# Half of a one-megabyte weight load is sent behind the last value block, and two row products trade places with a turned sum

## The chip, the cores and the metric

The kernel runs on one core of a Trainium2 chip, in one launch. Its time is the device time of one execution in microseconds (us). One execution was also recorded by the hardware profiler. Times inside the trace are counted from the first recorded instruction, and the span runs to the last one.

## The reference

One token goes through two branches that are mixed by a gate `g`:

```
g   = sigmoid(sum(x * gate_w))
q   = x @ wq                                  # 32 heads of 128, x has 512 elements
p   = softmax(q . k_cache / sqrt(128))        # 4096 cached keys for each head
a   = (p . v_cache).reshape(4096) @ wo        # 4096 -> 512
h   = relu(x @ w1 + b1) ** 2                # 512 -> 1376
b   = h @ w2 + b2                             # 1376 -> 512
out = g * a + (1 - g) * b                     # 512 numbers, bf16
```

Both branches read the same `x`. Keys and values are 32 MB each in bf16, and with the weights the core reads 78 MB. Nothing is reused, so every byte is brought in once.

## The kernel before

**Blocks.** The 32 heads are handled in 8 groups of 4. For each group there is a key block K0 to K7 and a value block V0 to V7 of 4 MB each. They pass through four slots of the tile `KV` in the order `K0 K1 V0 K2 K3 V1 K4 V2 K5 K6 V3 K7 V4 V5 V6 V7`. V7 alone is brought in as four transfers of 1 MB with a semaphore each (`V_PARTS`), so that its products can start on the first quarter. Each part is 8 KB in each of 128 partitions.

**The queue.** Nearly all transfers are issued by SyncE (SP), written out by hand in the function under `@block.sync`. The end of that list is what the change edits. Before it, `load_w2(0)` is issued just ahead of V7. It brings rows 0 to 7 of `w2a`, 8 KB for each partition. After V7 come `wob` (rows of `wo` for the last eight heads, 1 MB), `wox` (128 KB, `wo` for head 23) and the three small pieces of `w2`:

```
W2_PARTS = [(0, 8), (FG, FG + 1), (8, 9), (9, 10)]
```

Here `FG` is 10. Pieces 0 to 9 are rows of `w2a` (a row is 128 x 512 weights), and piece `FG` is the remainder `w2b` with 96 partitions. `w2` is thus ten full parts and a short one, and each entry of `W2_PARTS` has its own semaphore `s_w2[n]`.

**The products at the end.** TensorE runs, in program order, `den(6)` and `pv(6)` (128 matmuls on V6), `mlp_out(0)` (32 matmuls on `w2a` rows 0 to 7), `den(7)` and `pv(7)` (128 matmuls on V7, a wait at each quarter), `regroup()` (a transpose and 16 small matmuls, with VectorE between them, that turn the last heads' outputs into columns), `out_b()` (32 matmuls on `wob`), `out_x()` (4 on `wox`) and `mlp_out(1, last=True)` (4 on `w2b`). All of these from `mlp_out(0)` on except `den`, `pv` and `regroup` add into `acc`, four columns of 128 numbers. When the last is done, VectorE adds the bias and writes `accs` (line 857).

**Turning the sum.** The output is wanted as 4 rows of 128. A matmul of `accs` with the identity turns the four columns into four rows in `acc4` (line 707, in 32-bit floats). Rows 8 and 9 of `w2` do not go through `acc`. `mlp_rows` (line 645) multiplies each of them with a diagonal arrangement `hd` of the hidden values, so that the result is in row form at once and adds into `acc4`. In the kernel before, row 8 is multiplied ahead of the turned sum and row 9 behind it. VectorE then casts `acc4` to `fin4` (line 859) and SP sends it out (line 349).

Of the kernel before, what the change touches and what calls it, by code (L numbers as in the profile page):

```python
# [5 lines left out]
def bass_gated_mix__gqa_block_cached__dense_activation_squared_relu__decode_kernel(  # L6
# [25 lines left out]
    FG = 10  # L32
# [28 lines left out]
    K_PARTS = [[4]] * NQ  # L61
    V_PARTS = [[4]] * (NQ - 1) + [[1, 1, 1, 1]]
    QF = 4
    W2_PARTS = [(0, 8), (FG, FG + 1), (8, 9), (9, 10)]
    INNER, OUTER, SEAM, WRAP = range(4)
    RUNS = [(INNER, 4, 12, 0, 2), (INNER, 4, 12, 1, 2),
            (OUTER, 4, 3, 0, 1), (SEAM, 7, 2, 0, 1), (OUTER, 9, 7, 0, 1),
# [18 lines left out]
    def turns():  # L86
        at, out = 0, []
        for _, e, k, _, _ in RUNS:
            d = (e - at) % 16
            out.append((False, d) if d != 1 else (True, e))  # L90
            at = (e + k) % 16
        return out
# [24 lines left out]
    with ctx:  # L117
        def sb(name, shape, dt):
            return ctx.enter_context(nc.sbuf_tensor(name, shape, dt))
# [4 lines left out]
        def sem(name):  # L124
            return ctx.enter_context(nc.semaphore(name))
# [31 lines left out]
        identf = sb("identf", [128, 128], fp32)  # L157
# [25 lines left out]
        accs = sb("accs", [128, 4], fp32)  # L183
# [18 lines left out]
        acc4 = pO[0:4, 128:256]  # L202
# [11 lines left out]
        s_w1 = sem("s_w1")  # L214
        s_w2 = [sem(f"s_w2{n}") for n in range(len(W2_PARTS))]
        s_wo = sem("s_wo")
# [54 lines left out]
        s_fin = sem("s_fin")  # L271
# [21 lines left out]
        @block.sync  # L293
        def _(eng):
            def load(dst, src, slot, parts, sems):
                at = 0
                for n, s in zip(parts, sems):
                    a, b = at * PB * 128, (at + n) * PB * 128
                    eng.dma_start(dst[:, slot, a:b], src[:, a:b]).then_inc(s, 16)
                    at += n  # L300

            def load_kv(n):
                kind, q = ORDER[n]
                if n >= 4:
                    done(*ORDER[n - 4])
                if kind == "K":
                    load(KV, k_q[q, :, :], n % 4, K_PARTS[q], s_k[q])
                else:
                    load(KV, v_q[q, :, :], n % 4, V_PARTS[q], s_v[q])

            def done(kind, q):
                if kind == "K":
                    eng.wait_ge(s_sd, q + 1)
                    eng.wait_ge(s_t, GQ * (q + 1))
                else:
                    eng.wait_ge(s_pv, q + 1)

            def load_first(n):
                if n == 0:
                    eng.wait_ge(s_qps, NQ)  # L320
                p, st, k, q = STRIPS[len(RUNS) + n]
                eng.dma_start(W2[p:p + st * (k - 1) + 1:st, :, :], woa_v[q:q + k, :, :],
                              max_dma_last_dim=16384).then_inc(s_wr, 16)

            def load_w2(n):
                a, b = W2_PARTS[n]
                if a < FG:
                    eng.dma_start(w2a[:, a:b, :], w2_v[:, a:b, :]).then_inc(s_w2[n], 16)
                else:
                    eng.dma_start(w2b[:, :], B_w2[FG * 128:F, :]).then_inc(s_w2[n], 16)  # L330

            for n in range(len(ORDER)):
                if n == len(ORDER) - 1:
                    load_w2(0)
                load_kv(n)
                if n == 2:
                    eng.wait_ge(s_z, 1)
                    eng.wait_ge(s_b2, 1)
                    eng.dma_start(w1_sb[:, :, :], w1_v[:, :, :]).then_inc(s_w1, 16)
                if 4 <= n < 4 + len(FIRST):  # L340
                    load_first(n - 4)
            done("V", NQ - 4)
            eng.dma_start(wob_sb, wob_v).then_inc(s_wo, 16)
            eng.dma_start(wox, A_wo[HX * 128:NA * 128, :]).then_inc(s_wx, 16)
            load_w2(1)
            load_w2(2)
            load_w2(3)
            eng.wait_ge(s_f4, 1)
            eng.dma_start(out[0, 0, :].rearrange("(j p) -> j p", p=128), fin4[:, :]).then_inc(s_out, 16)

# [116 lines left out]
        def _(eng):  # L467
# [138 lines left out]
            def regroup():  # L606
                eng.wait_ge(s_on, NQ)
                eng.transpose(KP[0][0:NH - NA, 0:128], onorm[:, NA:NH], ident[:, :]).then_inc(s_oT, 1)
                eng.wait_ge(s_oc, 1)
                for c in range(16):  # L610
                    mm = eng.matmul(O2B, selB[:, c // 8, c % 8, :], oB[:, TB * c:TB * c + TB],
                                    start=(c == 0), stop=(c == 15))
                mm.then_inc(s_oT, 1)

            def out_b():
                eng.wait_ge(s_o2, 1)
                eng.wait_ge(s_wo, 16)
                for t in range(TB):
                    for j in range(4):
                        eng.matmul(acc[:, j:j + 1], wob_sb[:, t, j * 128:(j + 1) * 128], o2B[:, t:t + 1],  # L620
                                   start=False, stop=False, skip_group_check=True)

            def out_x():
                eng.wait_ge(s_wx, 16)
                for j in range(4):
                    eng.matmul(acc[:, j:j + 1], wox[:, j * 128:(j + 1) * 128], onorm[:, HX:HX + 1],
                               start=False, stop=False, skip_group_check=True)

            def mlp_out(c, last=False):
                eng.wait_ge(s_w2[c], 16)  # L630
                a, b = W2_PARTS[c]
                for n in range(a, b):
                    M = 128 if n < FG else FR
                    w = w2a[:, n, :] if n < FG else w2b[:, :]
                    for j in range(4):
                        mm = eng.matmul(acc[:, j:j + 1], w[:, j * 128:(j + 1) * 128], hs[0:M, n:n + 1],
                                        start=False, stop=last, skip_group_check=True)
                if last:
                    mm.then_inc(s_acc, 1)

            def mlp_rows(c):
                eng.wait_ge(s_w2[c], 16)
                n = W2_PARTS[c][0]
                for j in range(4):
                    mm = eng.matmul(acc4, hd[:, n - 8, 4 * j:4 * j + 4], w2a[:, n, j * 128:(j + 1) * 128],
                                    start=(n == 8 and j == 0), stop=(n == FG - 1 and j == 3),
                                    skip_group_check=True)
                return mm

# [49 lines left out]
            pv(NQ - 1)  # L699
            regroup()  # L700
            out_b()
            out_x()
            mlp_out(1, last=True)
            eng.wait_ge(s_hs, 3)
            mlp_rows(2)
            eng.wait_ge(s_as, 1)
            eng.matmul(acc4, accs[:, :], identf[:, :], start=False, stop=False, skip_group_check=True)
            mlp_rows(3).then_inc(s_fin, 1)


        @block.vector
# [179 lines left out]
```

## Time and profile before

| what | value |
|---|---|
| median of 3 runs | 193.93 us (193.81 to 194.0) |
| the profiled execution's own time | 193.83 us |
| its span, first to last instruction | 192.4 us |
| mean granted TensorE clock | 0.689 |
| busy share of TensorE, VectorE, ScalarE | 66%, 66%, 52% |
| HBM read | 78.32 MB, 407 GB/s over the span |
| DMA engines' mean busy share from 172.16 to 185.41 us | 1.01 |
| the same from 185.41 to 189.28 us | 0.53 |
| the same from 189.28 us to the end | 0.00 |

The profiled execution took 1.43 us more than its span, which lies outside the recorded instructions. It is 0.10 us below the median. The shares of the engines are averages over the whole span. For the change only the last 20 us count, and there the table's last three rows say how far the transfers, and not an engine, set the pace.

### The profile page before, as it was taken

The numbers are of one execution on the slowest core, as the hardware profiler recorded it, in microseconds if no ns is written. First come the engines' busy times: TensorE is split into PE (matmuls) and PEld (weight loads), VectorE is DVE, ScalarE is ACT, GpSimd is POOL, SyncE is SP. The second block draws the span as 40 slices with busy tenths as digits, with TensorE's granted clock in tenths as the row PEclk, the third lists the DMA queues.
The fourth block names the chain that finished last, engine by engine and source line by source line (L and its number), as shares of the span: only waits on it lengthen the run. The fifth ranks groups of instructions, "written<-read, shape, count | busy, mean of one in ns | idle before, by whom it ended". The sixth has DMA issues, their size and how long they took to land.

```text
span 192.4 us, 6533 instructions
## 1 busy us (share of the span) xinstructions
PE 126.4 (66%) x2439; PEld 112.6 (59%) x2441; DVE 127.9 (66%) x1120; ACT 99.2 (52%) x214; POOL 19.8 (10%) x37
## 2 busy tenths in 40 slices
PE   0049498784689946384992659278789385755646
PEld 0023376563679946374982659178689384655645
DVE  1340399999607899999989459999989981100001
ACT  3006489799502898457398029869809935000000
POOL 5000000019964300000000000000000000000000
PEclk9999759699555576755597558858856955555555
DMA  6999999999999999999999999999999999999990
GB/s 225 437 429 436 436 438 426 436 401 451 426 424 433 436 433 422 434 433 426 404 426 426 417 433 436 414 424 433 431 433 426 429 421 433 426 380 421 417 341 18
DMA packets 4975, 78.73 MB, mean 409 GB/s; under 512 B 1334, under 2 KB 1816, under 8 KB 1817
## 3 DMA queue, kind: packets, MB, share of 16 engines
q1 hardware_dynamic: 3906, 75.76, 92.8%
q0 software_dynamic: 1024, 2.56, 3.4%
q8 instruction: 19, 0.31, 0.7%
q14 instruction: 12, 0.09, 0.1%
q10 hardware_dynamic: 14, 0.01, 0.0%
HBM read 78.32 MB, written 0.00 MB: 407 GB/s over the span
## 4 chain that ended last, share of the span: by engine, by line
DMA 43%; PE 22%; DVE 17%; ACT 12%; issue 4%; SPq 1%; ACTq 0%; DVEq 0%
DMA KV<-in_A_k_cache_dram 29%; DMA KV<-in_A_v_cache_dram 14%; DVE KV L773 13%; ACT kT L418 8%; PE KP L504 6%; PE pO L548 6%; PE pQ L486 3%; ACT E L436 2%; PE pQ L561 2%; ACT qb L407 2%; PE pS L516 1%; DVE w_sb L748 1%; PE pQ L557 1%; PE pO L539 1%; DVE S L773 1%
## 5 line engine op out<-in xcount | busy, mean ns | idle before, releaser
L773 DVE CUSTOM_DVE_ANT_0 KV<-KV,qb 128x128 bf16<-128x128 bf16 x512 | 110.2, 282 | 13.7 <-DMA KV<-in_A_k_cache_dram 13.7
L418 ACT ACTIVATE kT<-KP 128x1024 bf16<-128x1024 bf16 x64 | 61.9, 1026 | 37.1 <-PE KP L504 35.7
L504 PE MATMUL KP<-ident,KV 128*128 128x128 bf16 x512 | 51.8, 271 | 5.6 <-DMA KV<-in_A_k_cache_dram 5.6
L504 PEld LDWEIGHTS KP<-ident,KV 128*128 128x128 bf16 x512 | 43.0, 125 | 7.7 <-DMA KV<-in_A_k_cache_dram 4.1
L773 DVE DVE_READ_ACCUMULATOR2_ANT S<- 128x1 f32 x512 | 39.8, 78 | 0.0
L516 PE MATMUL pS<-qcol,kT 128*128 128x4 bf16 x512 | 23.5, 168 | 24.2 <-ACT kT L418 23.7
L516 PEld LDWEIGHTS pS<-qcol,kT 128*128 128x128 bf16 x512 | 20.9, 103 | 27.0 <-ACT kT L418 26.8
L548 PEld LDWEIGHTS pO<-E,KV 128*128 128x128 bf16 x1024 | 29.4, 105 | 7.9 <-DMA KV<-in_A_v_cache_dram 7.1
L548 PE MATMUL pO<-E,KV 128*128 128x4 bf16 x1024 | 29.1, 166 | 7.4 <-DMA KV<-in_A_v_cache_dram 6.6
L436 ACT ACTIVATE E<-S,nM 32x128 bf16<-32x128 f32 x32 | 18.4, 576 | 1.0
L407 ACT ACTIVATE qb<-pQ 32x128 bf16<-32x128 f32 x20 | 5.4, 268 | 13.1 <-PE pQ L486 12.8
L795 DVE RECIPROCAL rden<-pO 128x4 f32<-128x4 f32 x7 | 1.2, 173 | 15.3 <-PE pO L548 15.3
L373 POOL DMA_DIRECT2D xb<-in_B_w_dram x9 | 5.4, 604 | 39.3 <-PE pQ L486 39.3
L424 ACT ACTIVATE S<-pS 32x64 f32<-32x64 f32 x32 | 6.9, 214 | 4.3 <-PE pS L516 3.7
L486 PE MATMUL pQ<-W,xb 128*128 128x512 bf16 x18 | 7.1, 534 | 1.7 <-ACT qcol L412 1.1
L436 ACT ACTIVATION_READ_ACCUMULATOR E<-S,nM 32x1 f32 x32 | 8.0, 250 | 0.0
L376 POOL DMA_DIRECT2D W<-in_A_wo_dram x14 | 7.9, 565 | 0.0
L476 PE MATMUL pO<-S,onesf 1*24 1x128 f32 x2 | 0.6, 409 | 9.4 <-DVE S L739 9.4
L801 DVE SCALAR_TENSOR_TENSOR onorm<-pO,gcol,rden 128x4 bf16<-128x4 f32 x8 | 1.8, 222 | 7.4 <-PE pO L548 7.1
L754 DVE TENSOR_SCALAR e<-ez 128x1 f32<-128x1 f32 x1 | 0.2, 154 | 8.5 <-ACT ez L445 8.5
L476 PEld LDWEIGHTS pO<-S,onesf 1*24 1x24 f32 x2 | 0.1, 116 | 9.5 <-DVE S L739 9.5
L528 PE MATMUL pM<-onesf,dg 1*128 1x1 f32 x16 | 3.6, 294 | 3.1 <-DVE dg L788 3.0
(108 smaller groups left out, 90.5 us busy)
## 6 DMA issues: line engine op xcount, KB each, us to landing
KV<-in_A_k_cache_dram SPq DMA_DIRECT2D x8, 4096.0 KB, 30.6
KV<-in_A_v_cache_dram SPq DMA_DIRECT2D x7, 4096.0 KB, 25.4
W<-in_A_wq_dram SPq DMA_DIRECT2D x1, 4096.0 KB, 12.2
KV<-in_A_v_cache_dram SPq DMA_DIRECT2D x4, 1024.0 KB, 23.2
W<-in_A_wo_dram POOLq DMA_DIRECT2D x2, 768.0 KB, 19.9
w_sb<-in_B_w_dram SPq DMA_DIRECT2D x1, 1376.0 KB, 11.7
w2a<-in_B_w_dram SPq DMA_DIRECT2D x1, 1024.0 KB, 30.8
KV<-in_A_wo_dram SPq DMA_DIRECT2D x1, 1024.0 KB, 28.7
```

What stands on the lines that cost most here:

```text
L373: eng.dma_start(dm[0:d, sent, :, 0:8], src[:, :, 0:8]).then_inc(s_dm[sent], 16)
L376: eng.dma_start(W2[p:p + st * (k - 1) + 1:st, :, :], woa_v[q:q + k, :, :], max_dma_last_dim=16384).then_inc(s_wp[n], 16)
L407: eng.activation(qb[rows(r), c, :], QR[c][rows(r), r * 128:(r + 1) * 128], ACT.Copy)\
L418: eng.activation(kT[:, n % NT, :], KP[n % 3][:, :], ACT.Copy).then_inc(s_ev, 1)
L424: eng.activation(S[rows(r), q % NS, 0:YQ], S2[rows(r), :, r], ACT.Copy).then_inc(s_cp, 1)
L436: eng.activation(E[rows(r), q % NE, :, r], S[rows(r), q % NS, :], ACT.Exp, bias=nM[rows(r), q:q + 1], scale=SCALE, accum_out=RS[rows(r), h ...
L486: mm = eng.matmul(QR[c], xb[:, t, :], wq_sb[:, t, c * 512:(c + 1) * 512], start=(t == 0), stop=(t == 3))
L504: mm = eng.transpose(KP[n % 3][:, y * 128:(y + 1) * 128], key(q, b), ident[:, :])
L516: mm = eng.matmul(pS[q % 2][:, R * c:R * c + R], kT[:, n % NT, y * 128:(y + 1) * 128], qcol[:, R * q:R * q + R], start=True, stop=True)
L548: mm = eng.matmul(O[:, R * q:R * q + R], KV[:, V_SLOT[q], b * 128:(b + 1) * 128], E[:, q % NE, COLUMN[b], :], start=(b == 0), stop=(b == N ...
L561: mm = eng.matmul(H[0:M, n:n + 1], lhs, xcol[:, t:t + 1], start=False, stop=(t == 3))
L773: ins = eng.tensor_tensor_reduce(key(q, b), key(q, b), qb[:, q, :], 1.0, 0.0, ALU.mult, ALU.add, S[:, q % NS, c:c + 1])
```

## The change

`w2a` rows 0 to 7 are no longer one transfer of 1 MB but two of 512 KB (4 KB for each partition). The first stays ahead of V7. The second is issued behind `wob` and ahead of `wox`. Its 16 matmuls move with it: `mlp_out(0)` keeps 16 of its 32 in front of `den(7)`, and a new `mlp_out(1)` with the other 16 stands between `out_b()` and `out_x()`. The numbers of the later entries of `W2_PARTS` rise by one. Also, row 9 of `w2` is now multiplied ahead of the turned sum, right behind row 8, and the turned sum is the last matmul of the kernel.

```
-    W2_PARTS = [(0, 8), (FG, FG + 1), (8, 9), (9, 10)]
+    W2_PARTS = [(0, 4), (4, 8), (FG, FG + 1), (8, 9), (9, 10)]
...
             eng.dma_start(wob_sb, wob_v).then_inc(s_wo, 16)
+            load_w2(1)
             eng.dma_start(wox, A_wo[HX * 128:NA * 128, :]).then_inc(s_wx, 16)
-            load_w2(1)
             load_w2(2)
             load_w2(3)
+            load_w2(4)
             eng.wait_ge(s_f4, 1)
...
             out_b()
+            mlp_out(1)
             out_x()
-            mlp_out(1, last=True)
+            mlp_out(2, last=True)
             eng.wait_ge(s_hs, 3)
-            mlp_rows(2)
+            mlp_rows(3)
+            mlp_rows(4)
             eng.wait_ge(s_as, 1)
-            eng.matmul(acc4, accs[:, :], identf[:, :], start=False, stop=False, skip_group_check=True)
-            mlp_rows(3).then_inc(s_fin, 1)
+            eng.matmul(acc4, accs[:, :], identf[:, :], start=False, stop=True,
+                       skip_group_check=True).then_inc(s_fin, 1)
```

In `mlp_rows` the `stop` flag of the matmuls becomes `False`, since the turned sum now closes the group.

More of the change, by code (lines that the diff above doesn't have):

```diff
@@ L645, in mlp_rows @@
                     mm = eng.matmul(acc4, hd[:, n - 8, 4 * j:4 * j + 4], w2a[:, n, j * 128:(j + 1) * 128],
-                                    start=(n == 8 and j == 0), stop=(n == FG - 1 and j == 3),
+                                    start=(n == 8 and j == 0), stop=False,
                                     skip_group_check=True)
```

## The prediction

> **What bounds the kernel now.** I read the chain of waits that ended last first, cut to the time from 157 us on. Its columns are start, length in us, and what the chain ran on.
>
> ```profile
> 158.90 26.47 DMA KV<-in_A_v_cache_dram
> 185.41 1.03 PE pO L548 x32
> ...
> 186.53 0.23 DVE onorm L801
> ...
> 187.39 0.60 PE pS L611 x16
> ...
> 188.25 1.00 PE pQ L620 x32
> ...
> 189.46 0.52 PE pO L645 x4
> 189.98 0.43 PE pO L707 x2
> 190.40 0.44 PE pO L645 x4
> ```
>
> The end hangs on the landing of V7's last quarter. From its start on TensorE at 185.41 a fixed row of work follows up to the cast at 190.87, which is 5.46 us. So an earlier V7 is worth something, until a later transfer becomes the last to be waited for. The list of DMA issues, asked for one issue at a time, gives these (the last number is us from issue to landing). They are `w2a` rows 0 to 7, V7's last quarter, `wob`, `wox`, `w2b`, row 8 and row 9.
>
> ```profile
> w2a<-in_B_w_dram SPq DMA_DIRECT2D x1, 1024.0 KB, 30.8
> KV<-in_A_v_cache_dram SPq DMA_DIRECT2D x1, 1024.0 KB, 26.5
> KV<-in_A_wo_dram SPq DMA_DIRECT2D x1, 1024.0 KB, 28.7
> KV<-in_A_wo_dram SPq DMA_DIRECT2D x1, 128.0 KB, 28.6
> w2b<-in_B_w_dram SPq DMA_DIRECT2D x1, 96.0 KB, 28.3
> w2a<-in_B_w_dram SPq DMA_DIRECT2D x1, 128.0 KB, 28.1
> w2a<-in_B_w_dram SPq DMA_DIRECT2D x1, 128.0 KB, 20.2
> ```
>
> With the issue times of SP's timeline (143.84, 158.90, 159.37, 159.84, 160.33, 160.81, 169.08) the landings are 174.64, 185.37 (the chain has 26.47), 188.07, 188.44, 188.63, 188.91 and 189.28. V6 lands at 172.16 and V7's first three quarters at 177.77, 180.14 and 182.62, in the same way. They land in the order of issue, 2.4 to 3.1 us for each MB, at a DMA share of 1.01: the queue is in order and full. Against this stands the timeline of TensorE (start, length, and in brackets the idle time before).
>
> ```profile
> 188.25 1.00 PE L620 MATMUL pQ<-o2B,KV 128*128 128x1 bf16 x32 [0.28 <-DVE o2B L854]
> 189.11 0.24 PE L626 MATMUL pQ<-onorm,KV 128*128 128x1 bf16 x4
> 189.22 0.24 PE L636 MATMUL pQ<-hs,w2b 96*128 96x1 bf16 x4
> 189.39 0.59 PE L645 MATMUL pO<-w2a,hd 128*4 128x128 bf16 x4
> 189.77 0.63 PE L707 MATMUL pO<-identf,accs 128*4 128x128 f32 x2
> 190.20 0.63 PE L645 MATMUL pO<-w2a,hd 128*4 128x128 bf16 x4
> ```
>
> There is no idle time from 188.25 on. Each small piece has landed before it is used, by 0.67 us (`wox`: 189.11 less 188.44), 0.59 (`w2b`), 0.48 (row 8) and 0.92 (row 9). These margins are what the change can eat.
>
> **Half of w2 behind V7.** `w2a`'s MB took the queue 174.64 - 172.16 = 2.48 us, so half of it takes 1.24. The last quarter lands at 185.37 - 1.24 = 184.13, and everything up to `out_b` moves with it: matmuls at 184.17, `out_b` at 188.25 - 1.24 = 187.01. `wob` lands at 188.07 - 1.24 = 186.83 and is in time. (By V7's last quarter, 2.75 us, the half would be 1.38. I take 1.24, since it is this transfer's own row.)
>
> Behind `wob` the half is paid back, and the landings return to their old times plus what one more transfer costs. Bounds for that come from the small ones. They land 0.37, 0.19, 0.28 and 0.37 us after the one ahead, while 128 KB at `wob`'s 2.70 us for each MB would take 0.34. So a transfer costs -0.06 to +0.03 us beyond its bytes. The largest excess in any row is V7's first quarter, 177.77 - 174.64 = 3.13 us against 2.38 for the second: 0.75. I take 0.03, since the new transfer goes to the same queue stretch as the small ones, and keep 0.75 for a rival. The new landings are 188.10 (rows 4 to 7), 188.47, 188.66, 188.94 and 189.31.
>
> Here a rule speaks against the change. The Trainium skill, page DMA: Bandwidth & Descriptors, "Rules for kernel authors", asks for transfers of at least 1 MiB, and "Anatomy of one DMA" gives each a fixed cost of about 2.0 us, measured for transfers issued by GpSimd. If that were paid in the queue, an estimate from that page is 2.0 us less the 0.41 us gained below: about 1.6 us slower. The trace does not agree for this queue, since the 96 KB of `w2b` land 0.19 us after `wox`.
>
> **The 16 matmuls on the path.** The 32 matmuls of `out_b` are issued within 189.11 - 188.25 = 0.86 us, so 16 of this shape take 0.43. Until now they lay in front of `den(7)`, where TensorE waits for V7 anyway. Now they count. `out_b` is through at 187.01 + 0.86 = 187.87, rows 4 to 7 land at 188.10, and at the 0.04 us between landing and first matmul (185.37 to 185.41) they start at 188.14. They run to 188.57. `out_x` takes 0.11 (189.22 less 189.11) to 188.68, `w2b` 188.66 + 0.04 = 188.70, plus 0.17 (189.39 less 189.22): 188.87. So TensorE is ready for row 8 at 188.87 and its weights at 188.94 + 0.04 = 188.98. Row 8 starts at 188.98 instead of 189.39: 0.41 us earlier.
>
> **Row 9 ahead of the turn.** Same matmuls, other order: rows, turn, rows was 1.48 us from 189.39 to the cast at 190.87, and the cast now waits for rows, rows, turn. Row 9 can start at 188.98 + 0.43 = 189.41 and lands at 189.31 + 0.04 = 189.35, so it does not wait. Its margin falls from 0.92 to 0.06 us, and that cover is the thin one: each further delay of row 9 beyond it counts in full. VectorE's `accs` ended at 189.66, just before the turn at 189.77, so its 0.16 us was covered by four matmuls and is now covered by eight. No gain is counted for that.
>
> **SP's queue.** The list gets one more issue. SP's issue of row 8 was held from 160.81 for 8.2 us and that of row 9 until 171.17, so the queue's room was full. One more transfer ahead moves the hold to an earlier piece and the last issue a few us on. Pieces that land at 188 cover that with 17 us. Nothing else is behind them on SP but the output.
>
> **The early part.** `w2a`'s first half lands at 173.40 and TensorE reaches it at 175.61 as before, behind `pv(6)`. There TensorE stood 2.03 us for no wait that shows, until 177.99, eight matmuls in. In the stream the same instruction follows the same number of others, so I leave that stop. Then 8 matmuls, `den(7)` and two quarters of V7 (2.15 us for 64) end near 180.8, before the third quarter lands at 181.38. The cover is 0.6 us.
>
> **The sum.** +1.24 (V7) - 0.43 (16 matmuls) = 0.81 on TensorE's own path, of which row 8's landing lets 0.41 through. The profiled execution's 193.83 becomes 193.42. The median before is 0.10 above it, so I give 193.52 for the median, rounded to 193.5.
>
> **Rivals.** *TensorE's own path decides.* If the last pieces come earlier than assumed (the 0.53 DMA share after 185.41 says that most engines are done by then and a few are late, so a slightly more even load would do it), the gain goes up to 0.81: 193.93 - 0.81 = 193.1. Against it: nothing in the change evens the load.
>
> *The extra transfer, or a late engine, holds up the queue behind V7.* Price 0.25 to 0.75 by V7's first quarter. Rows 8 and 9 come later by as much, and the gain falls to 0.16 or turns into a loss of 0.34: 193.8 to 194.3. For it: the thin margin of row 9. Against it: the four small landings. The page's rule above stands beside this one.
>
> *TensorE's instruction supply stops it in V7's last quarter.* This is the rival on the slower side. The stops at 136.52 and 142.57 us (0.27 and 0.76 us, marked "issue") lie 128 matmuls apart, 6.05 us. The one at 177.99 lies 5.6 us behind matmul 8 of V6's 128, again 128 back. The next such place is in V7's last quarter, after about 6 of its 32 matmuls before, and after 22 now, because 16 are gone from in front of it. TensorE reached it at 185.6, 7.6 us after 177.99, without a stop. Now it comes there at 184.8, 6.8 us after. If the supply needs more than that, the stop is on the path. It costs nothing up to 0.4 us (the landings cover that), and the change is a loss from 0.81 us, so from a supply of 7.6 us on. A stop of 2.03 us would give 193.93 + 2.03 - 0.81 = 195.15. Against it: 5.6 and 6.05 are below 6.8.
>
> *V7 comes no earlier*, so the queue is not in order: 193.9 or a little more. All eleven landings speak against it.
>
> **How the numbers follow.** A run of this kernel can tell about 0.2%, 0.39 us, from no change, and the forecast of 0.41 lies on that border. Its own range is a gain of 0.25 to 0.55, 193.4 to 193.7. Chances: forecast 0.50 (0.30 of it faster by over 0.2%, 0.20 within), TensorE's path 0.17 (faster), held-up queue 0.23 (0.19 within, 0.04 slower), supply 0.06 (slower), no earlier V7 0.04 (within). That makes 0.47 faster, 0.43 within, 0.10 slower. The range runs from 193.1, the whole 0.81, to 193.95, a loss of nothing. It leaves out the supply and the worse part of the held-up queue.
>
> **What would show it.** V7's last quarter starts on TensorE near 184.2. `out_b` starts near 187.0 with no wait for `wob`. A wait of about 0.3 us for a DMA stands ahead of the new 16 matmuls, and row 8 starts at 189.0, set by its landing. Landings of rows 8 and 9 within 0.1 us of 188.94 and 189.31 confirm the price of the extra transfer. The prediction is wrong if row 9 lands after 189.4, if "issue" stands in V7's last quarter, or if V7 moves by less than 1 us.

## The result and the profile after

The changed kernel takes 193.60 us (median of 20 runs) against 193.93 us for the kernel before (20 runs). The ratio is 0.9983 with a 95% interval of 0.9977 to 0.9990, so it is faster by 0.33 us, or 0.19 to 0.45 us. The forecast was 0.41. The gain lies inside the 0.2% that was called the border in the prediction, and it is clear of zero. The profiled execution took 193.59 us at a span of 192.2 us.

The chain of waits of the changed kernel shows what took V7's place (start, length in us, what it ran on).

```profile
160.96 27.32 DMA w2a<-in_B_w_dram
...
188.32 0.59 PE pQ L637 x16
...
189.12 0.12 issue
189.24 1.01 PE pO L646 x8
190.25 0.44 PE pO L710 x2
...
190.72 0.28 DVE fin L862
```

In this execution it no longer goes through V7. ("issue" is time in which the engine waited for nothing that the profile shows.) The second half of `w2` is the transfer the chain ends on, and then the two rows of `w2` and the turned sum follow. The DMA issues, one at a time, in the order V7's last quarter, `wob`, rows 4 to 7, `wox`, `w2b`, row 8, row 9 (last column: us to landing):

```profile
KV<-in_A_v_cache_dram SPq DMA_DIRECT2D x1, 1024.0 KB, 24.1
KV<-in_A_wo_dram SPq DMA_DIRECT2D x1, 1024.0 KB, 26.3
w2a<-in_B_w_dram SPq DMA_DIRECT2D x1, 512.0 KB, 27.3
KV<-in_A_wo_dram SPq DMA_DIRECT2D x1, 128.0 KB, 27.2
w2b<-in_B_w_dram SPq DMA_DIRECT2D x1, 96.0 KB, 26.9
w2a<-in_B_w_dram SPq DMA_DIRECT2D x1, 128.0 KB, 18.9
w2a<-in_B_w_dram SPq DMA_DIRECT2D x1, 128.0 KB, 18.7
```

SP's timeline has the issues at 160.01, 160.48, 160.96, 161.43, 161.91, 170.19 and 170.73. So they land at 184.11, 186.78, 188.26, 188.63, 188.81, 189.09 and 189.43. The column has one decimal, so these sums are good to 0.05 us. The landing records of the traces have two decimals, and where hundredths matter below, the text says that a landing is from them. In this execution V6 landed 0.21 us later than in the one before (its first matmul starts at 172.38 instead of 172.17), ahead of everything that was changed. Where these two traces are compared below, that is taken off. V7's last quarter is 1.45 us earlier in that count, and the small pieces are where they were: row 8 lands 16.72 us behind V6 (16.75 before) and row 9 17.06 (17.12 before). One trace is good to some tenths only: in a second trace of the changed kernel, shown further down, V7's last quarter is 1.89 us earlier against V6, and row 8 lands 16.29 us behind it.

The timeline of TensorE in the same execution (PEld is its weight load):

```profile
184.17 1.24 PE L549 MATMUL pO<-E,KV 128*128 128x4 bf16 x32 [1.46 <-DMA KV<-in_A_v_cache_dram]
184.98 0.34 PEld L549 LDWEIGHTS pO<-E,KV 128*128 128x128 bf16 x10 [0.15 <-issue]
...
187.22 1.02 PE L621 MATMUL pQ<-o2B,KV 128*128 128x1 bf16 x32 [0.26 <-DVE o2B L857]
188.31 0.51 PEld L637 LDWEIGHTS pQ<-hs,w2a 128*128 128x128 bf16 x16 [0.17 <-DMA w2a<-in_B_w_dram]
188.32 0.59 PE L637 MATMUL pQ<-hs,w2a 128*128 128x1 bf16 x16
...
188.88 0.24 PE L637 MATMUL pQ<-hs,w2b 96*128 96x1 bf16 x4
...
189.24 1.01 PE L646 MATMUL pO<-w2a,hd 128*4 128x128 bf16 x8
...
190.05 0.63 PE L710 MATMUL pO<-identf,accs 128*4 128x128 f32 x2
```

Before, the last 16 matmuls of `w2a` rows 0 to 7 were not in this picture at all. Now they stand at 188.32, just behind their landing, and row 8 stands 0.15 us behind its own (0.14 by the landing records, which have it at 189.10). Inside V7's last quarter there is a short stop marked "issue", with 10 of the 32 weight loads behind it.

### The profile page after: what moved, and what is told of

The parts are those of the page before. It is cut to its first block, busy times and chain, and to the rows that moved or that the text cites. A ratio compares the mean times of both kernels' runs of the same rounds, so it can differ in the third digit from the quotient of the medians.

```text
span 192.2 us, 6534 instructions
## 1 busy us (share of the span) xinstructions
PE 124.2 (65%) x2439; PEld 111.4 (58%) x2441; DVE 129.0 (67%) x1120; ACT 99.3 (52%) x214; POOL 19.9 (10%) x37
## 4 chain that ended last, share of the span: by engine, by line
DMA 48%; DVE 23%; PE 12%; ACT 10%; issue 4%; SPq 1%; DVEq 0%; ACTq 0%
DMA KV<-in_A_k_cache_dram 34%; DVE KV L776 19%; DMA w2a<-in_B_w_dram 14%; ACT kT L419 6%; PE KP L505 6%; PE pO L549 2%; ACT E L437 2%; PE pQ L487 1%; DVE w_sb L751 1%; PE pS L517 1%; DVE S L776 1%; SPq L299 1%; PE pO L646 1%; ACT qb L408 0%; ACT S L425 0%
## 5 line engine op out<-in xcount | busy, mean ns | idle before, releaser
L776 DVE CUSTOM_DVE_ANT_0 KV<-KV,qb 128x128 bf16<-128x128 bf16 x512 | 112.0, 285 | 14.6 <-DMA KV<-in_A_k_cache_dram 14.6
L505 PE MATMUL KP<-ident,KV 128*128 128x128 bf16 x512 | 51.0, 268 | 6.4 <-DMA KV<-in_A_k_cache_dram 6.4
L505 PEld LDWEIGHTS KP<-ident,KV 128*128 128x128 bf16 x512 | 42.5, 123 | 8.6 <-DMA KV<-in_A_k_cache_dram 4.1
L525 PE MATMUL pM<-identf,mp 128*1 128x128 f32 x8 | 3.0, 372 | 4.2 <-DVE mp L784 4.2
```

The costliest lines, as they stand in the source:

```text
L505: mm = eng.transpose(KP[n % 3][:, y * 128:(y + 1) * 128], key(q, b), ident[:, :])
L776: ins = eng.tensor_tensor_reduce(key(q, b), key(q, b), qb[:, q, :], 1.0, 0.0, ALU.mult, ALU.add, S[:, q % NS, c:c + 1])
```

## Experiments

Medians are compared with runs of the kernel before on the same chip, whose medians were 193.91, 193.84, 193.84 and 193.81 in the four groups of runs.

**Which of the two edits.** The first kernel keeps the split and puts row 9 back behind the turned sum (in `mlp_rows` its last matmul gets the `stop` flag back):

```
...
-            mlp_rows(4)
             eng.wait_ge(s_as, 1)
-            eng.matmul(acc4, accs[:, :], identf[:, :], start=False, stop=True,
-                       skip_group_check=True).then_inc(s_fin, 1)
+            eng.matmul(acc4, accs[:, :], identf[:, :], start=False, stop=False, skip_group_check=True)
+            mlp_rows(4).then_inc(s_fin, 1)
```

> The changed kernel with row 9 of w2 put back behind the turned sum, so only the split and the move of half of w2 remain. If the landing of row 8 sets the end (the account of the prediction), row 9 is not waited for in either place and the time is that of the changed kernel, 193.6 us. If the new order of row 9 and the turned sum brought the gain, the time is that of the kernel before, 193.93 us.

It took 193.59 us, ratio 0.9981 (0.9972 to 0.9990). The other edit alone, in the kernel before (without the `stop` flag in `mlp_rows`):

```
...
             eng.wait_ge(s_hs, 3)
             mlp_rows(2)
+            mlp_rows(3)
             eng.wait_ge(s_as, 1)
-            eng.matmul(acc4, accs[:, :], identf[:, :], start=False, stop=False, skip_group_check=True)
-            mlp_rows(3).then_inc(s_fin, 1)
+            eng.matmul(acc4, accs[:, :], identf[:, :], start=False, stop=True,
+                       skip_group_check=True).then_inc(s_fin, 1)
```

> The kernel before with only row 9 ahead of the turned sum. If the landing of row 8 sets the end: no change, 193.93 us, since row 9 lands at 189.28 and is wanted at 189.82. If the order brought the gain: 193.6 us.

It took 193.87 us, ratio 0.9999 (0.9990 to 1.0008). The gain belongs to the move of half of `w2`. The new order of row 9 and the turned sum does nothing that these runs can tell: its interval, 0.19 us faster to 0.16 us slower, holds zero.

**What sets the end now: TensorE's work or the landings.** Two kernels take away one of the two at a time. The first leaves the 16 matmuls out, and the output lacks them. The transfer and the wait for it stay:

```
             out_b()
-            mlp_out(1)
+            eng.wait_ge(s_w2[1], 16)
             out_x()
```

> The changed kernel without the 16 matmuls of the second half of w2 (the output lacks them); its transfer and the wait for it stay. If landings set the end, row 8 is waited for all the same and the time falls by 0 to 0.1 us from the changed kernel's 193.6. If TensorE's own path sets it, it falls by the 16 matmuls, 0.43 us, to 193.2.

It took 193.49 us, ratio 0.9980 (0.9971 to 0.9988): 0.10 us below the kernel with the split alone on the same chip, and nothing near the 0.43 us of the work left out. Its timeline shows where the time went.

```profile
187.26 1.01 PE L621 MATMUL pQ<-o2B,KV 128*128 128x1 bf16 x32 [0.26 <-DVE o2B L857]
188.52 0.24 PE L627 MATMUL pQ<-onorm,KV 128*128 128x1 bf16 x4 [0.25 <-DMA KV<-in_A_wo_dram]
...
189.04 1.01 PE L646 MATMUL pO<-w2a,hd 128*4 128x128 bf16 x8
```

TensorE now waits for `wox` instead, and row 8 starts at 189.04 behind its landing (188.91 by the landing records). The second kernel leaves the transfer out and keeps the work: its 16 matmuls wait for nothing and read the first half of `w2` again, so the output is wrong by that.

```
             eng.dma_start(wob_sb, wob_v).then_inc(s_wo, 16)
-            load_w2(1)
...
-                    w = w2a[:, n, :] if n < FG else w2b[:, :]
+                    w = w2a[:, n - 4 if c == 1 else n, :] if n < FG else w2b[:, :]
```

> The changed kernel without the transfer of the second half of w2; its 16 matmuls read the first half again (the output is wrong by that), so TensorE's work is unchanged. If landings set the end, the pieces behind V7 land 1.24 us earlier, TensorE's own path decides, and the whole 0.81 us against before shows: 193.1 us. If TensorE's own path sets the end of the changed kernel already, nothing changes: 193.6.

It took 193.22 us (7 runs), ratio 0.9965 (0.9952 to 0.9978), 0.69 us below the kernel before. In its trace row 8 lands at 187.98 (188.03 by the landing records) and waits for TensorE, which is never idle for a transfer behind V7:

```profile
184.71 1.02 PE L548 MATMUL pO<-E,KV 128*128 128x4 bf16 x32 [2.24 <-DMA KV<-in_A_v_cache_dram]
...
187.52 1.01 PE L620 MATMUL pQ<-o2B,KV 128*128 128x1 bf16 x32 [0.26 <-DVE o2B L857]
...
189.11 1.01 PE L646 MATMUL pO<-w2a,hd 128*4 128x128 bf16 x8
```

So both predictions of the landing account come out: work taken away gives 0.10 us, and bytes taken away give 0.37 us more than the split alone on the same chip, though the intervals of these two overlap a little. The 0.81 us of TensorE's own path was not reached. The interval, 0.43 to 0.93, includes it. The trace can't decide that: its execution took 193.50 us, above the median, and V7's last quarter starts at 184.71 in it, 0.54 us later than in the changed kernel, though the queue up to there is the same.

**All eight rows behind V7.** If half is good, is the whole better?

```
-    W2_PARTS = [(0, 4), (4, 8), (FG, FG + 1), (8, 9), (9, 10)]
+    W2_PARTS = [(0, 0), (0, 8), (FG, FG + 1), (8, 9), (9, 10)]
```

with the early `load_w2(0)` and `mlp_out(0)` removed.

> The changed kernel with all eight rows 0 to 7 of w2 sent behind V7 in one transfer, and their 32 matmuls behind out_b. V7 should land 2.48 us earlier than in the kernel before. If the landing of V7 set the end, the time would fall by 2.48 - 0.86 = 1.6 us to 192.3. If the pieces behind it set it, the eight rows land at 188.10 in the times of before, their 32 matmuls run to 188.96, w2b's to 189.24, and row 8 starts at 189.24 instead of 189.39: 193.8 us, slower than the changed kernel.

It took 193.73 us, ratio 0.9992 (0.9983 to 1.0001).

```profile
182.91 1.01 PE L547 MATMUL pO<-E,KV 128*128 128x4 bf16 x32 [1.46 <-DMA KV<-in_A_v_cache_dram]
...
188.09 1.01 PE L635 MATMUL pQ<-hs,w2a 128*128 128x1 bf16 x32 [1.35 <-DMA w2a<-in_B_w_dram]
...
189.24 1.01 PE L644 MATMUL pO<-w2a,hd 128*4 128x128 bf16 x8
```

V7 comes 2.5 us earlier than in the kernel before, and nearly all of that turns into a wait of 1.35 us and a burst of 32 matmuls. Row 8, landed at 188.92, starts at 189.24, the time that was written down for it. Here an early V7 is worth nothing that can be told, since the pieces behind it are the last to come.

**The price of a transfer.** The half goes in four transfers of 128 KB:

```
-    W2_PARTS = [(0, 4), (4, 8), (FG, FG + 1), (8, 9), (9, 10)]
+    W2_PARTS = [(0, 4), (4, 5), (FG, FG + 1), (8, 9), (9, 10), (5, 6), (6, 7), (7, 8)]
```

with `load_w2(5)` to `(7)` and `mlp_out(5)` to `(7)` beside number 1.

> The changed kernel with the second half of w2 sent as four transfers of 128 KB instead of one of 512 KB, each with its own wait; same bytes, same matmuls. If a transfer costs the queue at most 0.03 us beyond its bytes, the time is 193.6 to 193.7 us. If each further transfer had a price of 0.75 us (the largest excess in the trace of before), three more would give 195.8; by the Trainium skill's page DMA: Bandwidth & Descriptors, section Anatomy of one DMA, with 2.0 us for each, an estimate is 199.6.

It took 193.79 us, ratio 0.9994 (0.9985 to 1.0003), which is more than expected from 0.03 us each and far from 0.75 or 2.0. So it was run again, with the changed kernel beside it on one chip:

> The changed kernel itself, run beside the next three on one chip, so that they can be compared with it directly: 0.3 us below the kernel before.

> The kernel with the second half of w2 in four transfers again, now beside the changed kernel. If three more transfers are free, as its landings say (row 8 and row 9 land 16.74 and 17.06 us behind V6, in the changed kernel 16.72 and 17.06), its time is that of the changed kernel within 0.1 us. If they have a price that the landings do not show, it is again 0.2 us above it.

The changed kernel took 193.49 us, ratio 0.9981 (0.9972 to 0.9989), and the one with four pieces 193.75, ratio 0.9993 (0.9985 to 1.0002). The difference came back: 0.26 us, or 0.09 us for each further transfer, though the two intervals still overlap. The traces do not show it as a price in the queue. From `wob`'s landing to row 9's, the stretch in which the further transfers land, the landing records have 2.55 and 2.64 us with four pieces, and 2.62 and 2.58 in the two traces of the changed kernel. Row 8 lands 16.74 and 16.89 us behind V6 in the two traces with four pieces, and 16.72 and 16.29 in the two of the changed kernel. That scatter is as large as the effect, so its cause stays open.

**The wait in front of row 8.** TensorE waits there for the hidden values, long ready, and then for row 8. The first wait is moved up:

```
+            eng.wait_ge(s_hs, 3)
             regroup()
...
-            eng.wait_ge(s_hs, 3)
             mlp_rows(3)
```

> The changed kernel with TensorE's wait for the hidden values (long fulfilled) moved from in front of row 8 to in front of regroup. Row 8 started 0.15 us after its landing in the changed kernel, where V7's last quarter starts 0.04 to 0.06 after its own. If the second wait in front of row 8 makes that difference, row 8 starts 0.05 us after its landing and the time falls by 0.1 us to 193.4 to 193.5; if not, the start stays at 0.10 to 0.16 us after it and the time stays at 0.33 us below the kernel before.

It took 193.53 us, ratio 0.9986 (0.9977 to 0.9995). The timeline:

```profile
183.96 1.03 PE L549 MATMUL pO<-E,KV 128*128 128x4 bf16 x32 [1.46 <-DMA KV<-in_A_v_cache_dram]
185.46 0.27 PE L609 MATMUL KP<-ident,onorm 128*8 128x128 bf16 x1 [0.47 <-DVE onorm L804]
...
188.86 1.01 PE L646 MATMUL pO<-w2a,hd 128*4 128x128 bf16 x8
```

By the landing records row 8 lands at 188.82, and it starts at 188.86, 0.04 us later. In six traces with the two waits in a row it started 0.13 or 0.14 us behind its landing. So the trace says yes. The transpose behind the moved wait now stands idle for 0.47 us instead of 0.38 or 0.39, so the price of the wait seems to have gone there, where row 8's landing covers it. The time says nothing: 0.28 us below the kernel before is no more than the changed kernel has, and 0.1 us is below what these runs can tell.

**A version meant to beat both.** If the last landing sets the end, what follows it should be short. Row 8 goes through the column sum (4 matmuls of one column), and row 9 comes in two transfers of 64 KB, so that half of its products can run ahead of the last landing:

```
-            load_w2(4)
+            eng.dma_start(w2a[:, 9:10, 0:256], w2_v[:, 9:10, 0:256]).then_inc(s_w2[4], 16)
+            eng.dma_start(w2a[:, 9:10, 256:512], w2_v[:, 9:10, 256:512]).then_inc(s_w9, 16)
...
                 for j in range(4):
+                    if j == 2:
+                        eng.wait_ge(s_w9, 16)
...
-            mlp_out(2, last=True)
+            mlp_out(2)
+            mlp_out(3, last=True)
             eng.wait_ge(s_hs, 3)
-            mlp_rows(3)
             mlp_rows(4)
```

> A version meant to beat both: row 8 of w2 goes through the column sum (4 matmuls of 1 column instead of 4 of 128), and row 9 comes in two transfers of 64 KB, so that half its products can run before the last landing. If landings set the end, row 9's second half lands at 189.34 and starts at 189.38, two matmuls take 0.21, the turned sum starts at 189.6 instead of 189.84: 0.2 us below the changed kernel, 193.4. If the turned sum then waits for accs, or 512-byte pieces are dearer, 193.6 or more.

It took 193.36 us, ratio 0.9973 (0.9964 to 0.9982). Then it ran again beside the changed kernel, together with a kernel that has only the first of its two parts:

> The version with both parts (row 8 in the column sum, row 9 in two transfers) again, beside the changed kernel: 0.15 to 0.2 us below it if half of row 9's products ahead of the last landing is what pays.

> The version meant to beat both with only one of its two parts: row 8 goes through the column sum, but row 9 comes in one transfer. If the last landing sets the end, row 9 still lands last, and its four matmuls and the turned sum still follow: no change from the changed kernel. If shorter work on TensorE is what pays, 0.2 to 0.3 us below it.

Both parts: 193.19 us, ratio 0.9968 (0.9958 to 0.9979), 0.30 us below the changed kernel on that chip, with intervals that just overlap. Row 8 in the column sum alone: 193.35, ratio 0.9976 (0.9966 to 0.9986). The timeline of the first:

```profile
188.91 0.27 PE L639 MATMUL pQ<-hs,w2a 128*128 128x1 bf16 x4
...
189.19 0.59 PE L650 MATMUL pO<-w2a,hd 128*4 128x128 bf16 x4
...
189.57 0.63 PE L714 MATMUL pO<-identf,accs 128*4 128x128 f32 x2
```

The halves of row 9 landed at 189.08 and 189.24, and the turned sum starts 0.33 us behind the last landing. In the changed kernel it is 0.62 us (189.43 to 190.05). That is the predicted effect and a little more. But in the changed kernel the turned sum does not wait for row 9: row 8 sets it, with its late start and eight matmuls. Counted from row 8's landing (landing records), the turned sum starts 0.95 and 0.94 us later in the two traces of the changed kernel, 0.86 with row 8 in the column sum, and 0.71 and 0.66 with both parts. The times have the same order, so the gain of 0.14 us with the first part alone, which was not expected, fits. Its interval overlaps that of the changed kernel almost wholly, though, so it may be nothing, and the share of each part is not shown. In the trace of the first part alone TensorE itself was late, behind a stop of 0.71 us in V7's last quarter.

## Why the prediction was right, point by point

**V7 comes earlier.** Forecast 1.24 us, measured 1.45 in the trace. `w2`'s half took 1.28 us (172.37 to 173.65), as written; V7's four quarters took 10.46 us instead of 10.73. The 1.89 us of the second trace say how much of such a difference is scatter.

**`out_b` at 187.01.** It started at 187.22, which is 187.01 with V6's 0.21 us taken off. The agreement hides two errors: V7 was 0.21 us earlier, and the stop in its last quarter took as much again. That the two cancel is luck.

**The instruction supply.** This rival came about, at its place and below its price. The prediction put the next stop behind about 22 of the 32 matmuls of V7's last quarter. The trace has 22 weight loads ahead of the stop and 10 behind it in the changed kernel. With that, one of the signs that were to say that the prediction is wrong came about: "issue" stands in V7's last quarter. In this trace it took 0.21 us, below the 0.4 us that the landings cover, so the sum held. The second trace of the changed kernel shows it larger (matmuls first, then three lines of its chain of waits):

```profile
183.88 0.72 PE L549 MATMUL pO<-E,KV 128*128 128x4 bf16 x21 [1.46 <-DMA KV<-in_A_v_cache_dram]
185.06 0.43 PE L549 MATMUL pO<-E,KV 128*128 128x4 bf16 x11 [0.46 <-issue]
...
188.18 0.56 PE L637 MATMUL pQ<-hs,w2a 128*128 128x1 bf16 x16
...
188.96 1.01 PE L646 MATMUL pO<-w2a,hd 128*4 128x128 bf16 x8
```

```profile
159.15 24.68 DMA KV<-in_A_v_cache_dram
...
188.95 0.00 issue
188.96 1.01 PE pO L646 x8
```

In seven traces of this family the stop shows, 0.15 to 0.78 us long in the weight loads, and in all of them the weight loads behind it start 6.38 or 6.39 us after those behind the stop in `mlp_out(0)` (178.59 and 184.98 in the changed kernel, 179.60 and 185.99 in the kernel with row 8 in the column sum). The size that failed is the 6.8 us that the prediction took as available: V7's last quarter came at 184.17, the stop in `mlp_out(0)` lasted to 178.59, and 0.6 us into the quarter that is 6.2. The times it set against that were too few: 5.6 was counted from a place without a stop, and beside the 6.05 other traces have up to 7.25 us from stop to stop over the same stretch of instructions (137.59 to 144.84 in the kernel with the new order alone). Before, 177.99 + 6.39 = 184.38 had passed long before matmul 6 of that quarter, at 185.6.

The traces also point to what the stop waits for. Their DMA records have a queue named "instruction" (q8) that moves 16 KB at a time. In the changed kernel two such transfers ran from 176.24 to 177.32 and from 182.44 to 183.46, and the two stops ended 1.27 and 1.52 us after them. In the seven traces this delay is 1.27 to 1.63 us. So 6.39 us is not a fixed need: with the wait ahead of `regroup`, a transfer ended at 183.17, and TensorE passed the same place at 184.55 without a stop, 1.38 us after it and 6.11 us after the stop in `mlp_out(0)`. The place itself goes by the count of instructions. In the kernel with all eight rows behind V7, other products stand there, and the stop is inside V7's first half, with 136 weight loads from V6's first up to it, where the changed kernel has 137:

```profile
178.26 1.62 PEld L547 LDWEIGHTS pO<-E,KV 128*128 128x128 bf16 x58 [1.62 <-issue]
```

In the second trace of the changed kernel the stop was large enough to bring TensorE's path level with the landings: rows 4 to 7 had landed at 187.97 (landing records), and their matmuls start at 188.18, when `out_b` is through. Its chain still goes through V7, and TensorE is ready for row 8 at 188.95, while row 8 landed at 188.82. The chain of the kernel with the split alone goes through V7 too. The Trainium skill, page Runtime: NRT & Kernel Launch, section "Instruction fetch mechanics", says that instructions come in blocks of 16 KiB, 256 of them, and that the cost of crossing a block is mostly hidden. The spacing agrees: 127 pairs of weight load and matmul and two waits that are instructions of their own lie between the two stops, and each transfer has 16 KB. "Mostly hidden" does not hold here, with the DMA engines busy (their mean share was 1.01 from 172.38 to 184.17): the stop in `mlp_out(0)` alone was 2.03 us before and 2.42 after.

**The half is paid back behind V7.** With the 0.21 us added, the forecast landings are 188.31, 188.68, 188.87, 189.15 and 189.52. Measured were 188.26, 188.63, 188.81, 189.09 and 189.43. The extra transfer's 0.03 us was not seen in that trace. By their times the kernels with three more transfers lose 0.09 us for each, and by their landings behind `wob` nothing. The rival of a held-up queue, with up to 0.75 us, did not come about behind `wob`, where the further transfers land, in any of these traces. The fixed cost of 2.0 us that the Trainium skill's page DMA: Bandwidth & Descriptors gives in "Anatomy of one DMA", measured for transfers issued by GpSimd, is not paid for each transfer in this queue: three more transfers cost 0.26 us together. Row 9 landed at 189.43, which is behind the 189.4 that was named as a sign of being wrong. V6's 0.21 us are in that, and without them it is 189.22.

**TensorE ready at 188.87, row 8 landing at 188.94.** Nearly level, and so they were: `w2b`'s matmuls start at 188.88, which with the 0.17 us of the forecast makes TensorE ready at 189.05, and row 8 lands at 189.09. The wait ahead of the new 16 matmuls, forecast at about 0.3 us, was 0.17, since the stop in V7 had made `out_b` later. The two kernels that take away work and bytes show on which side the end hangs: mostly on the landing, with TensorE's path close behind or level.

**The sum.** Forecast 0.41. In the trace the cast starts 18.34 us behind V6's first matmul instead of 18.70: 0.36. The 0.05 that lack are the difference of two errors. The term that was mis-sized is the 0.04 us from a landing to its first matmul: for row 8 it was 0.14 by the landing records, 0.10 more, since two waits stand in a row there. Row 8's landing, 0.05 us earlier than forecast, gave half of that back. The median's 0.33 agrees within its interval.

**Row 9's thin margin.** It was 0.06 us on paper and about 0.2 in the trace, where row 8 came later and row 9 earlier than forecast. It did no harm: the kernel that keeps row 9 behind the turned sum has the same time.

## What to carry to other kernels

When a queue is full to the end, moving bytes behind the critical transfer only moves the end as far as the last landing lets it. Work out both paths, the engine's and the landings', and take the later one: here 0.81 us of lead became 0.33. From then on it pays to shorten what follows the last landings, here with less work on row 8 and with row 9 in two pieces, so that half of its work is done before the second lands. The two together gave 0.30 us more. Bringing the large transfer earlier still gave nothing that can be told from no change.

## What was not expected of the hardware

By these traces TensorE's instructions come in DMA transfers of 16 KB on a queue of their own, and with the DMA engines at a mean share of 1.01 the engine can stand and wait for them. No run here changes those transfers themselves. The places go by the count of instructions: 127 pairs of weight load and matmul and two separate waits lie from one to the next at the end of this kernel. In seven traces such a stop ended 1.27 to 1.63 us after the transfer, and stops of up to 2.42 us show in the traces of the changed kernel. A change that makes data come earlier can uncover one. And a wait that is long fulfilled is not free when it stands in front of another: row 8 started 0.13 or 0.14 us behind its landing with two waits in a row, and 0.04 with one.
